# Attention, squared-ReLU layer and expert layer in one kernel: weight conversion from step 26, and some copies of transposed probabilities on VectorE

## The chip, the cores and the metric

The kernel runs on one core of one Trainium2 chip. The metric is the device time of one execution in microseconds, and the median over executions is what is compared. The engines are called as the profile calls them: PE is TensorE (PEld its weight loads), DVE is VectorE, ACT is ScalarE, POOL is GpSimd, and SP is SyncE, whose queue issues nearly all DMAs. Each of the engines works through its own instructions in the order in which they were written into its queue; a scheduler settles that order when the program is built.

## The reference

Three layers follow one another. The first is attention over 4 batches of 8 heads, 576 positions and 64 columns a head, where a block of 64 queries sees its own block of keys and the earlier ones. The second multiplies by `w_in`, squares the positive part and multiplies by `w_out`. The third sends each token to one of 8 experts.

```python
scores = scale * np.matmul(q, k.transpose(0, 1, 3, 2))
mask = block_i >= block_j                  # blocks of 64 positions
attn = np.exp(scores - max) / (sum + 1e-09)
x = np.matmul(attn, v)                     # (4, 8, 576, 64) -> 2304 tokens x 512
h = x @ w_in                               # 512 -> 2048
x = (s * np.maximum(h, 0) ** 2 + b) @ w_out
e = argmax(x @ w_gate + modality_bias[modality_id])   # 8 experts, 512 -> 1024 -> 512
out = gate * (np.maximum(x @ w1[e], 0) @ w2[e])
```

## The kernel before

**Attention.** A unit is a pair of heads of one batch: 16 units, each of 9 query blocks. `attention` is a generator that goes through 144 steps, one for each unit and block, and some steps more to drain. In a step it writes down the scores of one block (`scores`, lines 123 to 149: matmuls into a PSUM bank `sc`, the row maximum `nm` on DVE in line 142, the exponentials on ACT in line 147), the normalisation of the block before (`normalise`: the reciprocal `rc` on DVE, the product on POOL in line 160), and the transposition of the probabilities of a block five steps back (`p_transpose`: transposes on PE in line 179 into a bank `tp`, and a copy to the tile `pt` in line 185). `pv` multiplies `pt` by `v`, seven steps behind the scores; its results are copied on ACT (line 204) and stored to `xT_d` (line 207). At steps 4, 5 and 6 of a unit the next unit's q and k are transposed and split in a high and a low part.

**PSUM banks.** In the first 36 steps (units 0 to 3) attention has all eight banks: 4 for scores, 3 for transposes, 1 for `pv` (`BANKS_0`). From step 36 on it has 3, 2 and 1 (`BANKS_A`), and the second layer has the other two.

**Conversion of weights.** The weights come as 64-bit floats. The generator `convert` (line 352) brings the first half of `w_in` and `w_out` in, 16 chunks of 512 KB. Each time it is asked, it issues the load of one chunk (`load_f64`, line 320, on SP, two buffers `wr`), turns the chunk loaded before into 32-bit floats (`to_f32`: three DVE instructions on the tile `f`, lines 329 to 331), copies the chunk before that to its high part on ACT (line 364), and subtracts to get the low part of the one before that on POOL (line 335). It is asked 19 times in all, at the steps that the table `CONV` lists. Its instructions are held behind the step's last row maximum, exponential and product.

**Pieces of the second layer.** `_beside` gives out the work on the first six blocks of 256 tokens in 40 pieces: for each block one that loads the tokens, one for each `hidden` (24 matmuls of line 377, then relu, square and split) and two that project (line 392). A piece is written down when the step has reached `PIECE_0 + emitted * PIECE_D`, when enough chunks have been converted (11 for the first block, all 19 calls for the others) and when the block's tokens are finished.

```python
for _ in range(CONV.count(step)):
    ...
    converted += next(conv, 0)
while (emitted < len(plan) and step >= PIECE_0 + emitted * PIECE_D
       and converted >= 4 * NA[plan[emitted]] + 3 and done >= ...):
    next(pieces)
    emitted += 1
```

After attention the rest of the second layer (`after`) and the experts follow, with instructions that the change doesn't touch.

Of the kernel before, what the change touches and what calls it, by code (L numbers as in the profile page):

```python
# [20 lines left out]
def attention(nc, tc, ctx, ps, ident, q, k, v, xT_d):  # L21
# [140 lines left out]
    def p_transpose(u, blocks):  # L162
        i0 = blocks[0]
        grp = int(i0 >= 4)
        if i0 == 4 * grp:
            st[u]["pt", grp] = pt.tile(([P, 4, 2, P], [P, 5, 5, P])[grp], F32, name=f"pt{grp}", tag=f"pt{grp}")
        out = st[u]["pt", grp]
        nch = i0 // 2 + 1
        jobs = []
        if grp == 0:  # L170
            jobs.append(([(i, c) for i in blocks for c in range(nch)], out[:, i0:i0 + 2, 0:nch]))
        else:
            for c0, c1 in ((0, min(4, nch)), (4, nch)):
                if c1 > c0:
                    jobs.append(([(i0, c) for c in range(c0, c1)], out[:, i0 - 4, c0:c1]))
        for lst, o in jobs:
            t = ps.t.tile([P, 512], F32, name="tp", tag="t")
            for e, (i, c) in enumerate(lst):
                nc.tensor.transpose(t[:, e * P:(e + 1) * P], st[u][i][0][:, c * P:(c + 1) * P], ident)  # L179
            src = t[:, 0:len(lst) * P]  # L180
            if grp == 0:
                src = src.rearrange("p (i c n) -> p i c n", i=2, n=P)
            else:
                src = src.rearrange("p (c n) -> p c n", n=P)
            P_COPY(nc, i0)(o, src)  # L185
        for i in blocks:
            st[u].pop(i)

# [31 lines left out]
    def at(t):  # L220
        return seq[t] if 0 <= t < len(seq) else (None, None)

    done = 0
    for t in range(len(seq) + LP + 1):
        u, i = at(t - LT)
        if i in (1, 3):
            p_transpose(u, [i - 1, i])
        elif u is not None and i >= 4:
            p_transpose(u, [i])
        u, i = at(t)  # L230
# [15 lines left out]
        u, i = at(t - LN)  # L246
# [3 lines left out]
        u, i = at(t - LP)  # L250
# [22 lines left out]
NPBUF = 6  # L273
PTBUF = 1
BANKS_0 = (4, 3, 1)
P_COPY = lambda nc, i: nc.scalar.copy


class SquaredRelu:
# [211 lines left out]
NH_A = 1  # L491
BANKS_A = (3, 2, 1)
WB_ENG = lambda nc: nc.vector
CONV = [8 + 4 * n for n in range(19)]
PIECE_0 = 50
PIECE_D = 2.8
WA_ENG = lambda nc: nc.gpsimd
PASSES = ((0, 0), (0, 1), (1, 0))

# [653 lines left out]
def kernel(  # L1153
# [33 lines left out]
    with ExitStack() as c2, ExitStack() as early:  # L1187
# [6 lines left out]
        for step, done in enumerate(attention(nc, tc, c2, banks, ident, q, k, v, xT_d)):  # L1194
            if step == per:
                early.close()
                banks.open(c2, tc, 1, *BANKS_A)
                ffn.banks(c2, "a", NH_A)
            for _ in range(CONV.count(step)):
                with ExitStack() as behind:  # L1200
                    for i in banks.last.values():
                        behind.enter_context(tc.issue_after(i.ins))
                    converted += next(conv, 0)
            while (emitted < len(plan) and step >= PIECE_0 + emitted * PIECE_D
                   and converted >= 4 * NA[plan[emitted]] + 3 and done >= H // 2 * (1 + (plan[emitted] * TB + TB - 1) // S)):
# [58 lines left out]
```

## Time and profile before

| | us |
|---|---|
| median of 3 runs | 938.83 (936.92 to 939.79) |
| the profiled execution, its own time | 937.27 |
| its span in the profile | 935.6 |
| PE busy | 901.0 (96%) |
| DVE busy | 591.9 (63%) |
| ACT busy | 520.5 (56%) |
| POOL busy | 210.9 (23%) |

The busy times are of the whole span. Attention's units 0 to 8 take its first 150 us, the other units run beside the second layer up to 330 us, and from there on attention is over. A matmul counts as busy from its start to its modelled end, so that a PE that is busy is not a PE at its peak.

### The profile page before, as it was taken

The page shows a single profiled execution, that of the slowest core. Times are in us where ns is not written, and L with a number is a line of the kernel's source. Part 1 is how long each engine was busy: PE and PEld are TensorE (multiplying, and loading weights), DVE is VectorE, ACT ScalarE, POOL GpSimd, SP SyncE. Part 2 cuts the span into 40 slices and gives each one's busy share as a digit, 9 for nine tenths or more (in the row PEclk, how much of TensorE's full clock was granted, in tenths as well). Part 3 has the DMA queues.
Part 4 walks back from the last instruction along what each step waited for, and adds up shares of the span by engine and source line. Part 5 has one row for each costly group of instructions (what it writes and reads, how often), then busy time and mean ns, then how long its engine had stood idle before and what let it go on. Part 6 is the DMA issues. An engine that isn't in the chain of part 4 may idle for free. (4 is left out here: it accounts for less than half of the span.)

```text
span 935.6 us, 16290 instructions
## 1 busy us (share of the span) xinstructions
PE 901.0 (96%) x5529; PEld 722.5 (77%) x5529; DVE 591.9 (63%) x1368; ACT 520.5 (56%) x1105; POOL 210.9 (23%) x319
## 2 busy tenths in 40 slices
PE   7979999999999999999999999999989999999995
PEld 5766777788878788999998888888467776766774
DVE  5988976463645446777344444445768887686772
ACT  6878786575757543333223322222378786776763
POOL 4666665142333200000000000002121322121110
PEclk9999999999999999999999999999999999999998
DMA  6565553322320233445022222115263696537400
GB/s 146 153 161 135 162 157 76 90 59 66 79 74 27 71 102 102 136 143 195 23 68 68 69 68 68 46 46 200 71 228 116 234 384 231 207 123 273 158 25 25
DMA packets 109477, 113.79 MB, mean 122 GB/s; under 512 B 62679, under 2 KB 80617, under 8 KB 109387
## 3 DMA queue, kind: packets, MB, share of 16 engines
q1 hardware_dynamic: 105579, 100.74, 34.4%
q0 software_dynamic: 3808, 11.94, 3.6%
q8 instruction: 46, 0.75, 0.3%
q14 instruction: 44, 0.36, 0.1%
HBM read 143.58 MB, written 19.80 MB: 175 GB/s over the span
## 5 line engine op out<-in xcount | busy, mean ns | idle before, releaser
L377 PE MATMUL ph<-xh,wih 128*128 128x256 f32 x576 | 163.0, 283 | 0.0
L377 PE MATMUL ph<-xh,wil 128*128 128x256 f32 x576 | 162.5, 282 | 0.0
L377 PE MATMUL ph<-xl,wih 128*128 128x256 f32 x576 | 162.3, 282 | 0.0
L160 POOL TENSOR_TENSOR p<-p,rc 128x64 f32<-128x64 f32 (+2 forms) x144 | 112.0, 785 | 136.0 <-DVE rc L159 69.8
L381 ACT ACTIVATE r<-ph 128x512 f32<-128x512 f32 x72 | 43.0, 597 | 163.2 <-PE ph L377 138.0
L382 DVE SCALAR_TENSOR_TENSOR r<-r,sc 128x512 f32<-128x512 f32 x72 | 55.8, 775 | 93.5 <-ACT r L381 92.8
L377 PEld LDWEIGHTS ph<-xh,wih 128*128 128x128 f32 x576 | 109.2, 190 | 3.6 <-ACT r L381 0.9
L377 PEld LDWEIGHTS ph<-xl,wih 128*128 128x128 f32 x576 | 109.2, 190 | 2.2
L377 PEld LDWEIGHTS ph<-xh,wil 128*128 128x128 f32 x576 | 109.3, 190 | 0.1
L142 DVE TENSOR_REDUCE nm<-sc 128x1 f32<-128x288 f32 (+8 forms) x160 | 70.8, 450 | 55.1 <-PE sc L140 44.8
L147 ACT ACTIVATE p<-sc,nm 128x288 f32<-128x288 f32 (+8 forms) x160 | 80.6, 507 | 22.3 <-DVE nm L142 8.9
L902 DVE TENSOR_TENSOR w1l<-raw,w1h 128x1024 fp32r<-128x1024 f32 x60 | 72.2, 1225 | 28.6 <-ACT w1h L901 28.1
L392 PE MATMUL px<-woh,gh 128*128 128x512 f32 x200 | 81.5, 407 | 0.0
L902 DVE TENSOR_TENSOR w2l<-raw,w2h 128x1024 fp32r<-128x1024 f32 x64 | 74.9, 1218 | 6.6 <-ACT w2h L901 6.3
L392 PE MATMUL px<-woh,gl 128*128 128x512 f32 x200 | 78.6, 394 | 0.0
L392 PE MATMUL px<-wol,gh 128*128 128x512 f32 x200 | 78.5, 392 | 0.0
L910 POOL DMA_INDIRECT xr<-x_d,gidx_e x2 | 2.3, 1130 | 317.4 <-DMA raw<-in_moe_w_dram 317.1
L901 ACT CAST w2h<-raw 128x1024 fp32r<-128x1024 f32 x64 | 66.3, 1053 | 11.9 <-PE py L993 11.1
L385 ACT ACTIVATE gh<-r,sc 128x512 fp32r<-128x512 f32 x72 | 52.2, 724 | 34.6 <-DVE r L382 34.6
L179 PE MATMUL tp<-ident,p 128*128 128x128 f32 x400 | 66.0, 280 | 5.3 <-POOL p L160 3.9
L901 ACT CAST w1h<-raw 128x1024 fp32r<-128x1024 f32 x60 | 61.9, 1051 | 13.9 <-PE ph L978 9.8
L185 ACT COPY pt<-tp 128x512 f32<-128x512 f32 (+3 forms) x128 | 61.8, 499 | 8.9 <-PE tp L179 8.3
(279 smaller groups left out, 1970.5 us busy)
## 6 DMA issues: line engine op xcount, KB each, us to landing
raw<-in_moe_w_dram SPq DMA_DIRECT2D x172, 512.0 KB
xr<-xT_d SPq DMA_DIRECT2D x19, 512.0 KB
wr<-in_moe_w_in_dram SPq DMA_DIRECT2D x16, 512.0 KB
wr<-in_moe_w_out_dram SPq DMA_DIRECT2D x16, 512.0 KB
row<-part_d SPq DMA_DIRECT2D x20, 256.0 KB
x_d<-row SPq DMA_DIRECT2D x18, 256.5 KB
xT_d<-x SPq DMA_DIRECT2D x16, 288.0 KB
raw_q<-in_q_dram SPq DMA_DIRECT2D x32, 128.0 KB
```

Of the source, the lines that this page charges most:

```text
L142: ps.last["max"] = nc.vector.tensor_reduce(nm[:, e:e + 1], sc[:, 0:w], AX.X, ALU.max, negate=True)
L147: ps.last["exp"] = nc.scalar.activation(pr[:, k0:k0 + w], scs[e][:, 0:w], AF.Exp, bias=nm[:, 0:1], accum_out=sm[:, e:e + 1])
L160: ps.last["scale"] = nc.gpsimd.tensor_mul(pr[:, 0:n], pr[:, 0:n], rc.to_broadcast([P, n]))
L179: nc.tensor.transpose(t[:, e * P:(e + 1) * P], st[u][i][0][:, c * P:(c + 1) * P], ident)
L185: P_COPY(nc, i0)(o, src)
L377: nc.tensor.matmul(ph[:, e], self.wi[p][w][:, c, e * P:(e + 1) * P], x[a][:, c], start=(n == 0), stop=(n == 3 * KC - 1))
L381: nc.scalar.activation(r, ph, AF.Relu)
L382: nc.vector.scalar_tensor_tensor(r, r, self.sc[:, 0:1], r, ALU.mult, ALU.mult)
L385: nc.scalar.activation(gh, r, AF.Identity, bias=self.sc[:, 1:2])
L392: self.nc.tensor.matmul(px, g[a][:, e, t * P:(t + 1) * P], self.wo[p][w][:, e], start=(first and e == 0 and n == 0), stop=(last and e == 1 ...
L901: self.nc.scalar.copy(ws[0][c], r)
L902: self.nc.vector.tensor_sub(ws[1][c], r, ws[0][c].bitcast(F32))
```

## The change

Three things change, all of them in the tables. `CONV` asks for chunks at steps 26, 29, 32, ... 80 where it was 8, 12, 16, ... 80. `PIECE_0` and `PIECE_D` start the pieces at step 59, one in 2.5 steps, where it was step 50 and one in 2.8. And `p_transpose` gives the copies of three kinds of block (the pair that begins at 2, the blocks 5 and 7) to DVE in units 0 to 3; the others stay on ACT.

```diff
-            P_COPY(nc, i0)(o, src)
+            P_COPY(nc, u, i0)(o, src)
...
-P_COPY = lambda nc, i: nc.scalar.copy
+P_COPY = lambda nc, u, i: nc.vector.tensor_copy if u < 4 and i in (2, 5, 7) else nc.scalar.copy
...
-CONV = [8 + 4 * n for n in range(19)]
-PIECE_0 = 50
-PIECE_D = 2.8
+CONV = [26 + 3 * n for n in range(19)]
+PIECE_0 = 59
+PIECE_D = 2.5
```

The order of instructions on DVE in unit 2, before (`nm` is the row maximum, `rc` the reciprocal, `f` a chunk in conversion, `wr` the chunk as loaded):

```order
L142 TENSOR_REDUCE nm<-sc 128x1
L158 TENSOR_SCALAR rc<-sm 128x1
L159 RECIPROCAL rc<-rc 128x1
L329 TENSOR_SCALAR f<-wr 128x512
L158 TENSOR_SCALAR rc<-sm 128x1
L330 SCALAR_TENSOR_TENSOR f<-wr,f 128x512
L159 RECIPROCAL rc<-rc 128x1
L142 TENSOR_REDUCE nm<-sc 128x1
L331 SCALAR_TENSOR_TENSOR f<-wr,f 128x512
```

The same place of the changed kernel:

```order
L142 TENSOR_REDUCE nm<-sc 128x1 x2
L156 TENSOR_SCALAR rc<-sm 128x1
L158 TENSOR_SCALAR rc<-sm 128x1
L185 COPY pt_605<-tp 128x512
L159 RECIPROCAL rc<-rc 128x1 x2
L158 TENSOR_SCALAR rc<-sm 128x1
L142 TENSOR_REDUCE nm<-sc 128x1
```

The conversion is gone from units 1 and 2, and a copy out of a `tp` bank stands between the maxima. Counted over DVE's whole order, units 1 to 8 held 1, 3, 2, 2, 2, 3, 2 and 1 chunks (by their last instruction) before, and hold 0, 0, 2, 3, 3, 3, 3 and 2 now; the copies number 1 in unit 0, 3 in each of units 1 to 3, and 2 in unit 4, which finishes unit 3's blocks.

DVE at the start of unit 6 in the changed kernel, where the chunks stand closest:

```order
L331 SCALAR_TENSOR_TENSOR f<-wr,f 128x512
L158 TENSOR_SCALAR rc<-sm 128x1
L142 TENSOR_REDUCE nm<-sc 128x1
L159 RECIPROCAL rc<-rc 128x1
L158 TENSOR_SCALAR rc<-sm 128x1
L329 TENSOR_SCALAR f<-wr 128x512
L159 RECIPROCAL rc<-rc 128x1
L142 TENSOR_REDUCE nm<-sc 128x1
L330 SCALAR_TENSOR_TENSOR f<-wr,f 128x512
L158 TENSOR_SCALAR rc<-sm 128x1
L142 TENSOR_REDUCE nm<-sc 128x1
L331 SCALAR_TENSOR_TENSOR f<-wr,f 128x512
```

Nearly every maximum there now stands behind one instruction of a chunk.

SP's queue at the end of a unit, before (V of a later unit, the store of `xT_d`, and the weights' loads):

```order
L67 DMA raw_v<-in_v_dram 128x4x64 x2
L68 DMA raw_v<-in_v_dram 64x2x64
L207 DMA xT_d<-x 128x576
L320 DMA wr<-in_moe_w_in_dram 128x4x256
L320 DMA wr<-in_moe_w_out_dram 128x1024
```

and in the changed kernel:

```order
L68 DMA raw_v<-in_v_dram 64x2x64
L320 DMA wr<-in_moe_w_in_dram 128x4x256
L207 DMA xT_d<-x 128x576
L320 DMA wr<-in_moe_w_in_dram 128x4x256
L67 DMA raw_q<-in_q_dram 128x4x64 x2
L320 DMA wr<-in_moe_w_out_dram 128x1024
L68 DMA raw_q<-in_q_dram 64x2x64
L67 DMA raw_k<-in_k_dram 128x4x64 x2
```

Three weight loads now stand between two V loads, and the third, which needs a free `wr` buffer, stands ahead of a part of q and of k.

On PE, the order of both kernels holds 72 matmuls of line 377 and 24 of line 392 ahead of unit 9. In unit 9 there were 103 and 48, and there are 72 and 48 now.

## Rows read from the trace of the kernel before

**Rows 1.** The page, share of the span by engine.

```profile
PE 901.0 (96%) x5529; PEld 722.5 (77%) x5529; DVE 591.9 (63%) x1368; ACT 520.5 (56%) x1105; POOL 210.9 (23%) x319
```

**Rows 2.** Busy time, from unit 9 on: stretch, its length, each engine, clock, DMA.

```profile
150.06:188.77 38.71, 37.69 (x246) 31.14 (x246) 18.94 (x54) 19.89 (x53) 9.87 (x25) 1.00 0.29 77
188.77:330.00 141.23, 141.01 (x973) 116.55 (x973) 71.75 (x230) 89.93 (x263) 46.08 (x85) 1.00 0.22 63
```

**Rows 3.** Busy time by unit, units 1 to 8, then units 3 to 8 together.

```profile
core 0: us, PE busy (x) PEld busy (x) DVE busy (x) ACT busy (x) POOL busy (x), PEclk, DMA share, GB/s
...
21.58:34.23 12.65, 12.10 (x92) 9.27 (x90) 10.61 (x39) 11.24 (x41) 7.07 (x15) 1.00 0.47 93
34.23:50.63 16.40, 13.32 (x95) 9.95 (x94) 15.68 (x46) 13.23 (x45) 10.89 (x17) 1.00 0.73 219
50.63:64.66 14.03, 12.88 (x85) 10.03 (x83) 11.38 (x39) 11.84 (x41) 10.05 (x17) 0.88 0.45 114
64.66:81.21 16.55, 14.84 (x99) 10.53 (x100) 13.15 (x43) 13.79 (x46) 11.10 (x18) 1.00 0.55 146
81.21:97.56 16.35, 14.95 (x107) 11.66 (x107) 14.77 (x43) 13.48 (x44) 10.88 (x17) 1.00 0.71 200
97.56:119.67 22.11, 20.08 (x137) 15.98 (x133) 19.67 (x50) 16.46 (x48) 12.78 (x18) 1.00 0.57 155
119.67:134.96 15.29, 14.88 (x104) 10.56 (x103) 12.79 (x39) 13.26 (x44) 9.50 (x16) 1.00 0.41 128
134.96:150.06 15.10, 14.71 (x110) 11.53 (x107) 11.35 (x39) 12.64 (x44) 11.28 (x18) 1.00 0.53 129
...
50.63:150.06 99.43, 92.34 (x633) 70.30 (x631) 83.11 (x251) 81.48 (x257) 65.59 (x99) 0.98 0.54 147
```

**Rows 4.** The conversion's own busy time (tile f): length, DVE, ACT, POOL.

```profile
21.58:34.23 12.65, 2.29 (x3) 0.62 (x1) 0.00 (x0) 1.00 0.47 93
34.23:50.63 16.40, 8.30 (x11) 1.25 (x2) 3.20 (x2) 1.00 0.73 219
81.21:97.56 16.35, 6.43 (x8) 1.36 (x3) 3.51 (x3) 1.00 0.71 200
...
134.96:150.06 15.10, 3.13 (x3) 1.23 (x2) 3.71 (x3) 1.00 0.53 129
21.58:50.63 29.05, 10.59 (x14) 1.87 (x3) 3.20 (x2) 1.00 0.62 164
50.63:150.06 99.43, 29.15 (x35) 8.13 (x13) 19.69 (x14) 0.98 0.54 147
```

**Rows 5.** Copies out of PSUM by shape, ACT's and DVE's, whole span.

```profile
L185 ACT COPY pt<-tp 128x512 f32<-128x512 f32 x64 | 37.4, 593 | 6.6 <-PE tp L179 6.2
L185 ACT COPY pt<-tp 128x384 f32<-128x384 f32 x32 | 15.0, 483 | 0.8 <-PE tp L179 0.6
...
L625 DVE COPY gx<-gt 128x512 f32<-128x512 f32 x9 | 6.2, 684 | 0.7 <-PE gt L623 0.7
...
L1028 DVE COPY sxT<-pts 128x256 f32<-128x256 f32 x4 | 1.7, 416 | 0.0
```

**Rows 6.** The conversion's instructions: duration in ns, least, median and most; waits.

```profile
L330 DVE SCALAR_TENSOR_TENSOR f<-wr,f x32: 666/693/1708, 24.6 to 437.7; 128x512 int32<-128x512 int32 x32
L331 DVE SCALAR_TENSOR_TENSOR f<-wr,f x32: 674/692/1394, 26.0 to 438.4; 128x512 int32<-128x512 int32 x32
...
  DMA wr<-in_moe_w_out_dram: 1.6, 2
```

**Rows 7.** Timeline of a stretch in unit 4: start, length, engine, instruction, wait.

```profile
66.46 1.49 POOL L335 TENSOR_TENSOR wil<-f,wih 128x512 fp32r<-128x512 f32 x1
...
66.91 1.59 DVE L330 SCALAR_TENSOR_TENSOR f<-wr,f 128x512 int32<-128x512 int32 x1
...
68.42 0.34 DVE L142 TENSOR_REDUCE nm<-sc 128x1 f32<-128x192 f32 x1
...
69.42 0.45 PE L140 MATMUL sc<-kh,qh 128*128 128x384 f32 x1 [1.11 <-ACT p L147]
```

## The prediction

> **What bounds the kernel now.** I read the page's first part, then busy time by stretch, then the conversion's own share of each stretch, then single instructions. PE is busy for 96% of the span [rows 1], but that mean covers two regimes. From 188.77 us to the end of attention at 330 it is busy for 141.01 of 141.23 us, and from 150.06 to 188.77 for 37.69 of 38.71 [rows 2]. There PE has a backlog, and the second layer's matmuls fill every gap of attention. Whatever makes units 0 to 8 shorter by an amount brings the whole backlog forward by that amount, if the same matmuls are done by then; the order shows that they are (72 of line 377 and 24 of line 392 ahead of unit 9 in both). So the question is how long units 1 to 8 take, and the edit touches exactly these.
>
> Their lengths differ much [rows 3]: unit 1 takes 12.65 us, unit 2 16.40, although both do the same attention and neither holds a piece. What differs is the conversion: DVE spends 2.29 us on it in unit 1 and 8.30 in unit 2 [rows 4]. In unit 2 DVE is busy for 15.68 of 16.40 us, 95.6%, more than any other engine in any of these units. That is a unit bound by DVE. In unit 1 ACT has 11.24 of 12.65 (89%), DVE 84%, and PE 12.10, its waits between matmuls partly hidden in that figure. In units 3 to 8 DVE has 83.11 of 99.43 us (84%), ACT 81.48, POOL 65.59: no engine is full, and chains through all of them set the pace.
>
> How a chunk costs time is seen in unit 4 [rows 7]. DVE's second instruction on a chunk takes 1.59 us, beside a POOL instruction of 1.49; the row maximum behind it starts only at 68.42; its exponential frees a score bank late, and PE's next scores show 1.11 us of idle time. The cost is the delay of a maximum, not DVE's time as such.
>
> **The price of conversion.** The slope between units 1 and 2 is (16.40 - 12.65) / (8.30 - 2.29) = 0.62 us of unit for each us of conversion on DVE [rows 3, 4]. With three and two banks the nearest pair is units 8 and 5, each with about 24 matmuls of line 377: (16.35 - 15.10) / (6.43 - 3.13) = 0.38. So late conversion seems cheaper than early conversion. The bounds of this price: 0 if it all fits in the 16.32 us that DVE idles in units 3 to 8, and 1 if DVE is full.
>
> **Step 1: units 1 and 2 lose their conversion.** They give up 10.59 us of DVE and 1.87 of ACT [rows 4]. At 0.62 that is 6.6 us. The floor is the other bound: if no unit gets below unit 1's 12.10 us of PE, the two come to 24.2 where they took 29.05, and the gain is 4.85. ACT's floor lies lower, at 11.24 - 0.62 = 10.6. I take -6.3, near the slope, because PE's figure contains waits for ACT that the copies below shorten.
>
> **Step 2: units 3 to 8 take it over.** All 16 chunks are still finished before unit 9, and cost DVE 10.59 + 29.15 = 39.74 us in all. Units 3 to 8 thus get 10.59 us more. At 0.38 that is +4.0. The order supports a low price in one way: in unit 6 one instruction of a chunk stands between any two maxima, where unit 2 had up to two. At a price of 1 it is +10.6.
>
> **Step 3: the copies.** A copy of 512 columns takes 593 ns on ACT, one of 384 takes 483; on DVE 512 columns out of PSUM take 684 and 256 take 416 [rows 5], so that 384 lie half way, at 0.55 (an estimate). Per unit ACT loses 2 x 0.593 + 0.483 = 1.67 us and DVE gains 2 x 0.684 + 0.55 = 1.92. In units 1 and 2 DVE is left with 8.32 and 7.38 us of other work [rows 3, 4], so 1.92 stays under 11 us and is covered by PE's and ACT's own work; without that cover it would be 3.8 us in the two. ACT at about 9 us is then no bound there. In unit 3 and the start of unit 4, five copies put 3.2 us on DVE and take 2.8 off ACT; with both engines at 81 to 84% these about cancel. I put the step at 0, between -1.7 (ACT's part at 0.62) and +3.2 (DVE's part at 1).
>
> The Trainium skill (VectorE: DVE Perf Modes, Specifications) says that ScalarE sits closer to PSUM and VectorE closer to SBUF, which speaks against this step; the rows agree in direction, 593 ns against 684. It would add 12 x 0.09 = 1.1 us of work, which the sum has in the two figures already.
>
> **Step 4: the clock.** In unit 3 the granted clock is 0.88 on average over 14.03 us [rows 3], that is (1 - 0.88) x 14.03 = 1.7 us lost if PE had been full, at 1.2 GHz instead of 2.4 for some 3.4 us. It follows the unit in which PE was idle longest, 3.1 of 16.40 us. With unit 2 shorter this idle time goes. PE is not full there, so I take -0.9, between 0 (it comes back in a later unit) and -1.7.
>
> **Step 5: the pieces.** The same 40 pieces come, with the first block's moved from unit 5 and 6 to 6 and 7. Between 150 and 188.77 us PE idles for 1.0 us [rows 2]; 31 fewer matmuls in one heap in unit 9 can win no more than that. I take 0.
>
> **Step 6: the queue.** Three weight loads now lie between two V loads on SP, and DVE waited for a load in 2 of 32 cases, 1.6 us [rows 6]. Behind a late load stand DVE's maxima, and behind those everything. The loads are asked for three steps ahead of their use now, four before, and the third of a unit waits for a `wr` buffer. A step is about 1.8 us (99.43 us for 54 steps [rows 3]), so a load has about 5.5 us instead of 7.4. I take 0, since the scheduler puts the conversion of each about as far behind the stores as it was; at the 0.8 us of one such wait in each of units 4 to 8 it would be +4.0.
>
> **The sum.** -6.3 + 4.0 + 0 - 0.9 = -3.2 us. The profiled execution took 937.27 us, 1.7 outside its span included, and would come to 934.1. The median of the runs shown is 938.83, 1.56 above it, which gives 935.6 for the median.
>
> **The rivals.** With p as the price per us of late conversion, the difference is -7.2 + 10.59 p. A measurement of this kernel can tell about 0.3%, 2.8 us, from no change. So p under 0.42 is faster, p over 0.94 slower, and all between is the same.
>
> *The gain is given back.* If the price in units 3 to 8 is the 0.62 of units 1 and 2, moving chunks is worth nothing: -6.3 + 6.6 - 0.9 = -0.6, or 938.2. For it: unit 4 took 16.55 us with two chunks and no piece, more than unit 5 with more conversion, so that the 0.38 rests on a scatter of 1.3 us [rows 3]; attention then has fewer banks to hide a late maximum. The floor of 12.10 in step 1 leads to the same place (-4.85 + 4.0 - 0.9 = -1.8, or 937.1). Against it: DVE's idle time there is 16.32 us.
>
> *DVE fills up behind POOL: slower.* In units 3 to 7 every unit with three chunks stands where unit 2 stood, plus copies or the second layer's work. DVE would have 83.11 + 10.59 + 3.2 = 96.9 us of work. At unit 2's share of 95.6% that takes 101.4 us, 2.0 more than now; at unit 6's share, 19.67 of 22.11 or 89.0%, it takes 108.9, 9.5 more, and the sum is -6.3 - 0.9 + 9.5 = +2.3. At a price of 1, the whole added conversion on the path, it is +3.4, or 942.2. It decides from a share under about 88.6%. For it: line 330's instruction takes 666 ns at best and 1708 at most, the long ones beside POOL [rows 6, 7], and POOL's low parts now lie in the same units. The Trainium skill (GPSIMD Engine Reference, 1. Specifications) says that GpSimd shares its SBUF interfaces with VectorE and contends with instructions that have two SBUF inputs; lines 330 and 331 are such, and unit 4 agrees. By that rule a denser conversion stretches its own instructions. Against it: units 3 to 8 hold 14 of the 16 low parts already [rows 4], so POOL's share hardly rises.
>
> *A late load* gives 935.6 + 4.0 = 939.6, and counts with the same.
>
> **Chances and range.** Faster as summed 0.45; given back, or a late load, 0.32; slower 0.23. The likeliest case is 935.6, with a range of its own of 931.5 to 936.0. The low end takes unit 2's share of DVE (+2.0), the slope whole (-6.6), the clock whole (-1.7) and PE's last microsecond (-1.0): 7.3 us less, 931.5. The high end of the slower case is 942.2. The range runs from 931.4 to 942.2.
>
> **What would show it.** In the profile of the changed kernel units 1 and 2 should take about 11.4 us each, or 12.1 at the floor. DVE should be busy for about 10 us in each, and for 95 to 97 in units 3 to 8, which should last 102 to 104 us, and its share should lie at 92 to 95%; a share under 89% means that the slower rival holds. The granted clock should be 1.00 in units 1 to 8. Unit 9 should begin about 3 us earlier, at 147, and everything behind it should be moved by the same. DVE's idle time for `wr` should stay under 2 us. The prediction is wrong if units 1 and 2 stay above 12.5 us, if PE's waits for exponentials grow in units 4 to 7 by more than 4 us in all, or if the backlog from unit 9 on no longer fills PE.

## The result, and the profile after

The changed kernel takes 945.01 us (median of 4 runs, 944.82 to 945.94) against 939.16 of the kernel before beside it (4 runs, 936.92 to 939.79): a ratio of 1.0068, interval 1.0053 to 1.0082, so 0.7% slower. In the five groups of experiments the kernel before ran 100 times more, with medians of 940.0 to 940.9; against these the loss is 4 to 5 us. Ratios are estimated over all runs and need not be the quotient of two medians. The changed kernel's profiled execution took 944.82 us with a span of 943.1. The span before was 935.6, in an execution of 937.27 us, some 3 us below the median of those 100 runs; so up to 3 us of what the two profiles differ by is scatter.

The page's shares of the whole span answer to [rows 1]:

```profile
PE 905.6 (96%) x5529; PEld 727.5 (77%) x5529; DVE 597.7 (63%) x1380; ACT 516.5 (55%) x1093; POOL 210.8 (22%) x319
```

The twelve copies are in DVE's count (1380, 1368 before) and gone from ACT's. Nothing else shows at this level. Busy time by unit of the changed kernel, units 1 to 8, then units 1 and 2 together, 3 to 8 together, and unit 9; columns as in [rows 3]:

```profile
22.82:35.36 12.54, 11.97 (x89) 8.99 (x88) 9.85 (x38) 9.83 (x37) 6.50 (x13) 1.00 0.26 69
35.36:48.46 13.10, 12.47 (x93) 9.58 (x92) 9.77 (x38) 10.39 (x38) 6.87 (x15) 1.00 0.62 169
48.46:63.63 15.17, 12.07 (x88) 8.73 (x86) 12.22 (x43) 11.45 (x40) 8.64 (x16) 1.00 0.44 114
63.63:83.54 19.91, 17.02 (x97) 12.76 (x97) 17.45 (x48) 13.78 (x43) 10.72 (x17) 0.83 0.52 147
83.54:100.72 17.18, 14.33 (x88) 10.67 (x88) 16.07 (x45) 13.80 (x44) 12.87 (x18) 0.90 0.65 176
100.72:120.42 19.70, 17.67 (x120) 14.42 (x119) 17.57 (x47) 14.41 (x46) 14.21 (x19) 0.91 0.68 185
120.42:142.50 22.08, 21.53 (x136) 16.32 (x135) 18.95 (x48) 16.22 (x49) 11.27 (x18) 1.00 0.51 139
142.50:158.48 15.98, 14.73 (x110) 12.19 (x111) 12.82 (x43) 12.94 (x44) 12.54 (x18) 1.00 0.48 123
22.82:48.46 25.64, 24.44 (x180) 18.58 (x179) 19.62 (x76) 20.22 (x73) 13.36 (x27) 1.00 0.44 120
48.46:158.48 110.02, 97.35 (x634) 75.09 (x633) 95.08 (x269) 82.60 (x257) 70.25 (x101) 0.94 0.55 149
158.48:192.12 33.64, 33.61 (x215) 27.33 (x214) 17.40 (x51) 18.41 (x52) 9.91 (x25) 1.00 0.33 89
```

A unit is counted from its first exponential. Units 1 and 2 take 25.64 us where they took 29.05 [rows 4]: 3.4 less. Units 3 to 8 take 110.02 where they took 99.43 [rows 3]: 10.6 more, with the same number of matmuls (634 and 633). Unit 9 begins at 158.48 instead of 150.06, and from there on PE is full or nearly so in both (in unit 9 for 33.61 of 33.64 us, and before for 37.69 of 38.71 [rows 2]). The rest of the program, from unit 9 on, takes 943.1 - 158.5 = 784.6 us, where it took 935.6 - 150.1 = 785.5. So the loss lies in units 3 to 8, but for 1.2 us ahead of unit 1, which begins at 22.82 instead of 21.58. The granted clock, 0.98 over these units before, is 0.94, and units 4, 5 and 6 show 0.83, 0.90 and 0.91.

DVE is busy for 95.08 us there, as forecast (95 to 97), but that is 86.4% of the stretch. It is not full. The start of unit 4 shows a part of what happens instead. The timeline of the changed kernel, some of its rows (start, length, engine, instruction, and in brackets the idle time before it and what ended it):

```profile
59.67 0.38 SPq L320 DMA_DIRECT2D wr<-in_moe_w_out_dram  x1
...
63.51 1.33 DVE L329 TENSOR_SCALAR f<-wr 128x512 int32<-128x512 int32 x1 [1.37 <-DMA wr<-in_moe_w_out_dram]
64.10 0.49 PE L137 MATMUL sc<-kf,qf 128*128 128x128 f32 x2 [1.80 <-ACT p L147]
64.87 0.69 DVE L330 SCALAR_TENSOR_TENSOR f<-wr,f 128x512 int32<-128x512 int32 x1
65.61 0.69 DVE L331 SCALAR_TENSOR_TENSOR f<-wr,f 128x512 int32<-128x512 int32 x1
66.53 0.54 DVE L185 COPY pt<-tp 128x384 f32<-128x384 f32 x1
66.98 0.55 DVE L142 TENSOR_REDUCE nm<-sc 128x1 f32<-128x128 f32 x2
67.21 1.09 PE L179 MATMUL tp<-ident,p 128*128 128x128 f32 x4 [1.45 <-DVE pt L185]
67.36 0.37 ACT L147 ACTIVATE p<-sc,nm 128x128 f32<-128x128 f32 x1 [1.62 <-DVE nm L142]
```

DVE stands idle for a chunk's load, works through the three instructions of that chunk, and only then comes to the copy of unit 3's probabilities and to the maximum. PE waits 1.45 us for the copy (its bank `tp` is one of two), ACT 1.62 us for the maximum. PE's wait of 1.80 us for an exponential is not the copies' doing: conversion alone, without copies, has it too, with 1.70 us (last section). And the clock falls just then. Busy time of the same kernel around that place and in the two later dips:

```profile
60.00:64.80 4.80, 2.24 (x20) 1.55 (x19) 3.43 (x11) 3.13 (x11) 3.50 (x6) 1.00 0.96 292
64.80:71.60 6.80, 5.35 (x25) 4.95 (x23) 6.40 (x17) 3.50 (x11) 3.71 (x6) 0.50 0.60 155
71.60:80.00 8.40, 7.78 (x51) 4.93 (x49) 7.46 (x22) 6.61 (x20) 4.12 (x6) 1.00 0.21 43
88.70:92.10 3.40, 3.40 (x15) 2.83 (x16) 3.40 (x10) 1.92 (x8) 2.98 (x4) 0.50 0.88 239
105.80:109.20 3.40, 3.40 (x15) 3.31 (x14) 3.21 (x10) 1.83 (x6) 2.65 (x5) 0.50 0.92 260
```

PE was busy for 2.24 of 4.80 us, and is then granted 1.2 GHz for 6.8 us. Units 4 to 6 hold 6.8 + 3.4 + 3.4 = 13.6 us at that level; before, one stretch of 3.4 us in unit 3 was all that units 1 to 8 held.

PE has two more waits of over 1.2 us in units 3 to 8, 1.91 and 2.03 us, both longer than the one for the copy, and by then the last copy on DVE is over (at 69.03 us). The one in unit 6 (timeline of the changed kernel, some of its rows):

```profile
101.21 1.48 POOL L335 TENSOR_TENSOR wol<-f,woh 128x512 fp32r<-128x512 f32 x1
...
101.57 1.66 DVE L330 SCALAR_TENSOR_TENSOR f<-wr,f 128x512 int32<-128x512 int32 x1
...
103.16 0.15 DVE L159 RECIPROCAL rc<-rc 128x1 f32<-128x1 f32 x1
...
103.45 1.65 POOL L160 TENSOR_TENSOR p<-p,rc 128x576 f32<-128x576 f32 x1 [0.76 <-DVE rc L159]
...
105.15 0.66 PE L179 MATMUL tp<-ident,p 128*128 128x128 f32 x4 [2.03 <-POOL p L160]
```

A chunk's instruction, 1.66 us long beside one of POOL, stands ahead of a reciprocal; POOL's product waits for the reciprocal, and PE's transposes wait 2.03 us for the product. PE's waits for exponentials and for products in units 4 to 7, of the kernel before and then of the changed one (us in total, times, longest):

```profile
PE sc L140 <- ACT p L147: 2.4, 3, 1.1
PE sc L137 <- ACT p L147: 0.7, 1, 0.7
...
PE tp L179 <- POOL p L160: 0.5, 1, 0.5
```

```profile
PE tp L179 <- POOL p L160: 4.8, 3, 2.0
PE sc L137 <- ACT p L147: 1.8, 1, 1.8
```

The waits for exponentials have become shorter, and those for products have grown by 4.3 us. Over units 3 to 8 the waits for products are 0.7 us in the kernel before and 5.8 in the changed one. In two runs of the next section they are 1.1 us (the pieces alone) and 6.1 (conversion alone): they come with the moved conversion, and not with the copies. Over units 0 to 8 the sums are 3.9 and 7.1 us, as the kernel before has one such wait of 1.86 us at the end of unit 2, the unit that held three chunks.

### The profile page after: what moved, and what is told of

Same layout as the page of the kernel before. It is cut to its first block, busy times and chain, and to the rows that moved or that the text cites. A ratio compares the mean times of both kernels' runs of the same rounds, so it can differ in the third digit from the quotient of the medians.

```text
span 943.1 us, 16293 instructions
## 1 busy us (share of the span) xinstructions
PE 905.6 (96%) x5529; PEld 727.5 (77%) x5529; DVE 597.7 (63%) x1380; ACT 516.5 (55%) x1093; POOL 210.8 (22%) x319
## 5 line engine op out<-in xcount | busy, mean ns | idle before, releaser
L386 DVE SCALAR_TENSOR_TENSOR gl<-r,sc,gh 128x512 fp32r<-128x512 f32 x72 | 53.9, 748 | 19.5 <-ACT gh L385 19.4
```

Source lines behind the costliest of these rows:

```text
L386: self.low_last = nc.vector.scalar_tensor_tensor(gl, r, self.sc[:, 1:2], gh.bitcast(F32), ALU.add, ALU.subtract)
```

## Experiments

The first theory was that the slower rival of the prediction is right: conversion moved late costs its whole time, and the copies nothing. Its rival was that the copies cost.

**The parts alone.** One kernel has the copies only, the other moved conversion and pieces only.

```diff
# copies alone: against the changed kernel
-CONV = [26 + 3 * n for n in range(19)]      # and PIECE_0, PIECE_D as before
+CONV = [8 + 4 * n for n in range(19)]
# conversion alone: against the changed kernel
-P_COPY = lambda nc, u, i: nc.vector.tensor_copy if u < 4 and i in (2, 5, 7) else nc.scalar.copy
+P_COPY = lambda nc, u, i: nc.scalar.copy
```

> The kernel before with the copies of the change alone (three kinds of block on VectorE in units 0 to 3). The first theory, that the conversion moved into units 3 to 8 costs the time, expects no change here, 938 to 940.5 us. The rival, that copies on VectorE hold up the row maxima behind them, expects most of the 6 us: 943 or more, with units 1 to 4 longer by 1 us each.

> The change without its copies: conversion from step 26, a chunk in three steps, and the pieces from step 59; all copies on ScalarE. The first theory expects 944 to 947 us, units 1 and 2 at about 13 us each and units 3 to 8 about 9 us longer than before. The rival of the copies expects at most 941.

Copies alone: 945.17 us against 940.03, ratio 1.0055 (1.0039 to 1.0071). Conversion alone: 942.28, 1.0019 (1.0006 to 1.0033). The first theory fell. The copies, put at 0, cost 5 us on the kernel before, and moved conversion with its pieces 2.

**No conversion on DVE.** In both kernels the three instructions of a chunk are left out, and the weights that it converts are zeros (`zero` is a tile that POOL fills once).

```diff
-            f32 = raw and (self.to_f32(raw[0], raw[1].shape[1]), *raw[1:])
+            f32 = raw and (zero.rearrange("p (c n) -> p c n", c=raw[1].shape[1]), *raw[1:])
```

> The kernel before, in which the three VectorE instructions on each chunk during attention are left out (the weights that are used are zeros; loads, ScalarE's and GpSimd's parts stay). If these instructions stand on the path at a price of 0.4 to 1 us for each of their 39.7 us, attention gets shorter until PE's own chain is the floor, about 12.5 us a unit and 14 us of the second layer: some 15 us less, about 924, and no dip of the clock in units 3 to 6. If they were covered, 936 or more.

> The changed kernel with the same three instructions left out. The first theory expects it within 2 us of the kernel before without them (about 922 to 926), since only the copies and the place of loads and pieces are then left between the two. The rival of the copies, and one that blames loads or pieces, expects it 4 us or more above.

Zero weights send the tokens to other experts, so that the totals (953.31 and 958.21) don't compare with the other kernels', only the stretch up to unit 9. It begins at 138.4 in the kernel before without conversion (150.1 with it) and at 144.9 in the changed one (158.5). DVE's work on conversion thus costs 11.7 us for 39.74 in the one, 13.6 for 42.21 in the other: 0.29 and 0.32 a microsecond, nearly the same in both kernels. Units 3 to 8 of the two runs, the kernel before and then the changed one:

```profile
48.07:138.41 90.34, 87.58 (x641) 68.97 (x640) 59.94 (x220) 81.38 (x258) 61.81 (x106) 1.00 0.65 172
49.15:144.89 95.74, 90.05 (x634) 69.65 (x633) 60.90 (x221) 81.33 (x256) 63.26 (x102) 1.00 0.65 173
```

Up to unit 9, 6.5 us stay between the two kernels with no conversion on DVE in either, 5.4 of them in units 3 to 8. The two totals, which have the same zero weights, differ by 4.9 us, as much as the whole change costs. The granted clock is 1.00 in both rows. So the change costs about its full price without a chunk in DVE's queue and without a dip of the clock. What is left between the two are the copies, the pieces, the loads, and conversion's part on ACT and POOL.

**Which copy, and whether it is DVE's time.** One kernel keeps all copies on ACT and gives DVE twelve row maxima of the same size on a fixed tile instead; the others move the copies of some kinds of block only.

```diff
# idle reductions: before, behind P_COPY
+            if u < 4 and i0 in (2, 5, 7):
+                nc.vector.tensor_reduce(dull, idle[:, 0:len(lst) * P + 64], AX.X, ALU.max)
# some kinds: before, with
+P_COPY = lambda nc, u, i: nc.vector.tensor_copy if u < 4 and i in (2, 5) else nc.scalar.copy   # or (7,)
```

> The kernel before with all copies on ScalarE, and 12 reductions of a constant tile added to VectorE's queue, nearly where the copies stood and about as long; nobody waits for their results. If the copies cost by filling VectorE's queue, this costs the 5 us that the copies cost (943 to 946). If they cost because the copy itself comes late and the transposed probabilities, the product with v and its result on ScalarE wait for it, this costs at most 2 us (938.5 to 942).

> The kernel before with the copies of pair 2 and block 5 on VectorE in units 0 to 3, whose copies came 1.6 us later than ScalarE's did with all three; block 7 stays on ScalarE. The theory of the late copy expects nearly the whole cost, 943 to 946 us. A cost that goes by the number of copies gives two thirds, 942.5 to 944.

> The kernel before with the copy of block 7 alone on VectorE in units 0 to 3, which came no later than ScalarE's. The theory of the late copy expects no cost, 938 to 941 us, or a gain. A cost by the number of copies gives a third, about 941.5 to 942.5.

Against 940.23: idle reductions 941.70 (1.0018, 1.0004 to 1.0033); pairs at 2 and blocks 5 941.01 (1.0013, 0.9999 to 1.0026); blocks 7 939.53 (1.0006, 0.9993 to 1.0020). DVE's time alone makes about a third of the 5 us (0.4 to 3.1 us by the interval). The kinds do not add up to it: 0.13% and 0.06% against 0.55%. So no kind of copy alone accounts for it.

**The clock, held up by more matmuls.** Two more score matmuls a block in units 3 to 8 of the changed kernel, into the bank that the real ones then overwrite.

```diff
+            for _ in range(2 if 3 <= u <= 8 and i >= 2 else 0):
+                nc.tensor.matmul(sc[:, 0:max(w, 256)], qh[...], kh[...], start=True, stop=True)
```

> The changed kernel with two more score matmuls ahead of each block's in units 3 to 8; the scores overwrite them, so results stay, and PE gets some 2.4 us more work a unit, 14 us in all. If the half clock of 13.7 us in units 4 to 6 is a cause of its own, worth up to 5 us more than before, the dips go and the time falls to 940 to 943 or stays, though work was added. If the clock only follows the waits and costs little, the time rises by 3 us or more, to 948 and up.

957.42 us (1.0193, 1.0167 to 1.0218). The dips of units 3 to 8 fell from 13.6 to 3.4 us, but the units grew from 110.0 to 121.9 us: matmuls ahead of the scores lie on the chain, although PE has idle time. The clock can be had so, but the matmuls cost more than it gives back.

**A late copy and `pv`.** With the copies and without, `pv` written down a step later.

```diff
-LAGS = (1, 5, 7)
+LAGS = (1, 5, 8)
```

> The twelve copies on VectorE as in the changed kernel, conversion and pieces as before, and the product with v (pv) written down one step later (8 steps behind the scores where it was 7), so that a late copy has a step more before pv, and behind pv ScalarE's copy of x, wait for it. If the copies cost because pv and the ScalarE copy wait for a late copy, the cost of the copies (5.2 us with pv at 7) should fall to 1 us or less against the next kernel, which has the same pv and all copies on ScalarE. If they cost because VectorE's maxima stand behind a copy, or by the clock, about 4 to 5 us should stay.

> The kernel before with pv written down 8 steps behind the scores, and nothing else: the control of the run with the copies. Neither theory has a price for it; an estimate is 940, within 2 us of before.

948.48 us with the copies (1.0078, 1.0061 to 1.0095), 942.75 without (1.0016, 1.0004 to 1.0027). The difference is still 5.7 us. That `pv` and the ACT copy behind it wait for the late copy is not the cause.

**A third load buffer; conversion earlier.**

```diff
# third buffer: after
-        bufs = dict(raw=2, cv=3, xr=1, x=nx, r=nr, g=ng)
+        bufs = dict(raw=3 if ph == "a" else 2, cv=3, xr=1, x=nx, r=nr, g=ng)
# earlier: before
-CONV = [8 + 4 * n for n in range(19)]
+CONV = [6 + 3 * n for n in range(19)]
```

> The changed kernel with three buffers for the weights as loaded (wr) beside attention, where it has two, so that the third load of a unit can be issued a chunk earlier. If late loads on SP's queue are a part of the loss, VectorE's idle time for wr (1.8 us in unit 3, 0.2 later) goes and unit 9 begins 2 us or more earlier than 158.5; the time is about 943. If the order on VectorE alone makes the loss, nothing changes: 944 to 946.

> The kernel before with conversion moved the other way: a chunk in three steps from step 6 to step 60, with copies and pieces as before. By the prices that the runs gave (0.34 us of time per us of conversion in units 1 and 2, 0.71 in units 3 to 8), moving the last three or four chunks, 7 to 10 us of VectorE, out of units 7 and 8 into the first units is worth 2.7 to 3.7 us: about 937 against 940. If the price does not depend on the unit, 939 to 941; by the price of the prediction (0.62 early, 0.38 late) it is 2 us slower, 942.

The third buffer: 945.22, as the changed kernel. Its load for the start of unit 4 is still issued only at 60.71 us, and DVE waits 1.92 us for it, so that late loads were not tested by it. Conversion earlier: 945.68 (1.0050, 1.0034 to 1.0067) where the measured prices gave 937. These prices (0.34 early, 0.71 late) had been read between the kernel before and conversion alone, which also moves the pieces; the run of the pieces alone, further down, shows that this misled.

**Where the copies lie, and the pieces alone.** The copies in units 0 to 2 of the changed kernel; in units 0 and 1, or 2 and 3, of the kernel before; and the third part of the change alone.

```diff
-P_COPY = lambda nc, u, i: nc.vector.tensor_copy if u < 4 and i in (2, 5, 7) else nc.scalar.copy
+P_COPY = lambda nc, u, i: nc.vector.tensor_copy if u < 3 and i in (2, 5, 7) else nc.scalar.copy   # or u < 2, u in (2, 3)
# pieces alone: before
-PIECE_0 = 50
-PIECE_D = 2.8
+PIECE_0 = 59
+PIECE_D = 2.5
```

> The changed kernel with the copies on VectorE in units 0 to 2 only, so that nearly none of them lies in a unit with conversion. If the copies cost where they share VectorE's queue with conversion, units 3 and 4 together, 35.1 us in the changed kernel and 31.6 with conversion moved and no copies, fall back to about 32, and the time to 942 to 943 (a cost of 0 to 1 over moved conversion alone). If the copies cost by themselves, three quarters of the 2.9 us stay: about 944.5.

> The kernel before with copies on VectorE in units 0 and 1, where VectorE has 0 and 1 chunks of conversion. If they cost beside conversion alone, 940 to 941 (0 to 1 us over before); if they cost by themselves, half of the 5.2 us of all four units: 943.

> The kernel before with copies on VectorE in units 2 and 3, where VectorE has 3 and 2 chunks of conversion. If they cost beside conversion alone, nearly all of the 5.2 us: 944 to 945; if they cost by themselves, half: 943. With a mean granted clock over the runs as in the kernel before (0.990) instead of that of all twelve copies (0.987), the order on VectorE is the cause and not the clock.

> The kernel before with the third part of the change alone: pieces from step 59, one in 2.5 steps. The prediction puts it at 0: 940 to 941. If the 24 matmuls that come later (in units 6 and 7 where they stood in 5 and 6) were cover that PE lacks in unit 5, it is slower by 1 to 2 us, with a dip of the granted clock more in units 4 to 6, and moved conversion by itself costs nothing.

Against 940.52: the changed kernel with copies in units 0 to 2 only, 942.16 (1.0021, 1.0009 to 1.0033), as conversion alone without any copy (942.28). So by the medians the three copies of unit 3's blocks cost 945.01 - 942.16 = 2.9 us (4.4 by the ratios 1.0068 and 1.0021), and the other nine nothing, to within some 2 us. On the kernel before, the copies of units 0 and 1 (one chunk there) cost 1.6 us (942.15, 1.0017), those of units 2 and 3 (five chunks) 3.3 (943.86, 1.0037); together they give the 5 of all. So a copy costs most in the units that hold chunks. That the chunks are the reason is not shown by this: two of unit 3's three copies, those of blocks 5 and 7, also come after step 36, when there are two `tp` banks and no longer three, and no run tells the one from the other. The mean granted clock of this last run is 0.9875, as with all twelve copies (0.9873), so that it does not part order from clock either. Pieces alone: 940.86 (1.0000, 0.9989 to 1.0012).

The traces agree with the medians only in part. Of pieces alone, of conversion alone (which has the same pieces), and of the changed kernel with copies in units 0 to 2, in this order, units 1 and 2 together and units 3 to 8 together:

```profile
21.56:50.81 29.25, 25.48 (x184) 19.21 (x183) 26.42 (x84) 24.46 (x84) 18.15 (x31) 1.00 0.65 166
50.81:153.97 103.16, 96.15 (x654) 73.49 (x652) 84.04 (x258) 82.18 (x256) 69.01 (x109) 0.98 0.56 147
```

```profile
21.04:46.47 25.43, 24.40 (x176) 18.47 (x175) 17.77 (x70) 22.74 (x79) 13.55 (x29) 1.00 0.42 114
46.47:153.49 107.02, 95.39 (x638) 72.83 (x637) 92.89 (x265) 83.62 (x261) 68.66 (x101) 0.97 0.56 154
```

```profile
23.21:48.80 25.59, 24.41 (x180) 18.55 (x179) 19.64 (x76) 20.18 (x73) 13.34 (x27) 1.00 0.42 112
48.80:156.46 107.66, 96.20 (x634) 73.73 (x633) 93.61 (x266) 83.11 (x259) 69.75 (x101) 0.95 0.57 154
```

The pieces alone make units 3 to 8 longer by 103.16 - 99.43 = 3.7 us, but with 654 matmuls done by unit 9 where there were 633, and from unit 9 on that kernel takes 783.1 us, not 785.5. Line 377's matmuls follow one another at 0.12 us in the timeline of the kernel before (94.41, 94.53, 94.64 us), so that 21 of them are worth 2.5, and 1.2 of the 3.7 is left. Against this control moved conversion takes 29.25 - 25.43 = 3.8 us from units 1 and 2. It adds 107.02 - 103.16 = 3.9 to units 3 to 8, with 16 matmuls fewer done; at equal matmuls that is 5.8, an estimate. The copies of units 0 to 2 add 0.6 there, those of unit 3 another 2.4. Ahead of unit 1 the copies of units 0 to 2 add 2.2 (23.21 against 21.04), which their median does not show; the profiled execution of that run, 945.02 us, was the slowest of its ten.

With the copies of unit 3 on ACT, the start of unit 4 reads thus (timeline of the changed kernel with copies in units 0 to 2):

```profile
64.54 0.43 DVE L329 TENSOR_SCALAR f<-wr 128x512 int32<-128x512 int32 x1 [2.28 <-DMA wr<-in_moe_w_out_dram]
...
65.58 0.48 ACT L185 COPY pt<-tp 128x384 f32<-128x384 f32 x1
...
66.22 1.09 PE L179 MATMUL tp<-ident,p 128*128 128x128 f32 x4 [0.72 <-ACT pt L185]
```

The chunk's load is late here too (2.28 us of idle time), but the copy doesn't stand behind it, and PE waits 0.72 us for it. With the copies in units 2 and 3 of the kernel before, the same place reads:

```profile
67.17 0.43 DVE L329 TENSOR_SCALAR f<-wr 128x512 int32<-128x512 int32 x1 [3.00 <-DMA wr<-in_moe_w_out_dram]
...
69.04 0.54 DVE L185 COPY pt<-tp 128x384 f32<-128x384 f32 x1
...
69.73 0.63 PE L179 MATMUL tp<-ident,p 128*128 128x128 f32 x4 [2.60 <-DVE pt L185]
```

So these rows, and those of the changed kernel further up, show one chain: load, chunk, copy, bank, transposes. On ACT the copy does not wait for the chunk. How much of the copies' price this chain makes, the rows do not say; the two runs without conversion on DVE, where it cannot occur, say that it is not all.

**The loads a call ahead.** Two loads run ahead of their conversion, in three buffers; conversion stays at its steps. It was put into the changed kernel and into the kernel before.

```diff
-        raw = f32 = high = None
-        for c in chain((c for p in pairs for c in self.chunks(pool, p)), (None, None, None)):
+        raw = f32 = high = soon = None
+        for c in chain((c for p in pairs for c in self.chunks(pool, p)), (None,) * 4):
...
-            raw = c and (self.load_f64(c[0]), *c[1:])
+            raw, soon = soon, c and (self.load_f64(c[0]), *c[1:])
...
-CONV = [26 + 3 * n for n in range(19)]       # before: [8 + 4 * n for n in range(19)]
+CONV = [23 + 3 * n for n in range(20)]       # before: [4 + 4 * n for n in range(20)]
...
-                   and converted >= 4 * NA[plan[emitted]] + 3 and done >= ...
+                   and converted >= 4 * NA[plan[emitted]] + 4 and done >= ...
```

> The changed kernel with each chunk loaded one call before (two loads ahead of their conversion, three buffers wr, one call more and the first at step 23), and conversion at the same steps. In the runs with copies in unit 3, VectorE stood idle 1.4 to 3.0 us for a load of w_out with a copy of unit 3 behind it in its queue, and TensorE's transposes waited 1.5 to 2.6 us for that copy. If this late load is what makes the copies of unit 3 cost 2.9 us, the idle time for wr and TensorE's wait behind it at the start of unit 4 go, unit 9 begins at about 155.5 instead of 158.5, and the time is 942 to 943. If the chunk's own work ahead of the copy is the cause, 944.5 to 945.5.

> The kernel before with the same loads a call ahead (first call at step 4, conversion at the same steps, copies on ScalarE). VectorE waits 1.6 us for wr there, in units 4 and 5: if these waits are on the path, 938.5 to 939.5 against 940.5, faster than both kernels; if they are covered, 940 to 941.

The changed kernel with it: 943.23 us (1.0040, 1.0027 to 1.0052, against 940.16), between the two expectations; the wait of 1.45 us for the copy is gone, PE's waits for products in units 3 to 8 have fallen from 5.8 to 1.4 us, the wait of 1.80 for the exponential has become 2.13, DVE still waits 1.7 us for one load, and unit 9 begins at 154.95. The kernel before with it: 933.54 us (0.9923, 0.9901 to 0.9946). That is faster than both kernels, 0.8% under the one and 1.2% under the other, and four times what its idle time for `wr`, 1.6 us, had promised. Its units 3 to 8:

```profile
50.54:146.24 95.70, 88.93 (x631) 69.65 (x630) 83.45 (x253) 81.22 (x258) 66.22 (x102) 0.98 0.57 151
```

They take 3.7 us less than in [rows 3], and DVE's list of waits there holds no `wr` any more; but in units 1 and 2 it has one of 1.5 us that was not there before. The idle time for `wr` is 1.5 us in all where it was 1.6, so that it doesn't explain the 6.6 us, and what does is not shown. Nor does the edit bring the two kernels together: with it in both, the change costs 943.23 - 933.54 = 9.7 us.

## Why the prediction was wrong

**The bound** was read rightly: from unit 9 on PE is full (33.61 of 33.64 us in unit 9), and the end follows the start of that unit.

**Where the sum failed.** It gave -3.2; by medians the change costs 945.01 - 940.52 = +4.5. Of these 7.7 us, steps 1, 2 and 4 together make 4.6 (conversion alone takes 942.28 - 940.86 = 1.4 us more than the pieces alone, where -3.2 was forecast), step 3 makes 2.7 and the pieces 0.3.

**Step 1** (-6.3) was mis-sized: -3.8 in the run of conversion alone, -3.4 in the changed kernel. The slope of 0.62 between two units did not hold. Units 1 and 2 stopped at 25.4 to 25.6 us with PE busy for 24.4, which is the step's own floor of 24.2 in PE's busy time and one microsecond of gaps. PE's figure was said to contain waits for ACT that the copies shorten; with them ACT's work fell from 22.74 to 20.22 us, and the two units took 25.64 instead of 25.43.

**Step 2** (+4.0) was right or somewhat low in size: +3.9 as the traces stand, 5.8 at equal matmuls, or 0.55 for each of the 10.59 us instead of 0.38. So late conversion is not cheaper than early, which is the rival in which the gain is given back. The wait behind it was another than the prediction named. It followed a chunk to a late maximum, a late exponential and PE's scores [rows 7]; in units 4 to 7 PE's waits for exponentials fell from 3.1 to 1.8 us. What grew are PE's waits for POOL's products, from 0.5 to 4.8 us, behind a reciprocal that stands behind a chunk.

**Step 3** (0, at most +3.2) is the step whose reasoning failed. The copies cost 945.01 - 942.28 = 2.7 us on top of moved conversion (4.6 by the ratios 1.0068 and 1.0019), and units 3 to 8 show 3.0. The copy's own time was right: 681 ns for 512 columns and 534 for 384, against 684 and 550. The argument was not. It weighed the copies as work only (3.2 on DVE, 2.8 off ACT, both at 81 to 84%), and work on DVE makes about a third of their price, as the twelve reductions show. The rows show one reason more. Behind a chunk whose load is late, a copy of half a microsecond holds a `tp` bank and a maximum, and PE and ACT wait 1.45 to 2.60 us. The prediction had asked of the chunks what stands behind them, but not of the copies what stands ahead of them. That this makes the whole price is not shown, and the runs without conversion on DVE speak against it. The step's own bound of +3.2 was in neither end of the range; with it the upper end of 942.2 would have been 945.4.

**Step 4** (-0.9) had the wrong sign. The dip of unit 3 went, as forecast, and 13.6 us of half clock came in units 4 to 6.

**Step 5** (0) holds for the time, 940.86 against 940.52; by the stretches it moves 3.7 us into units 3 to 8 and 2.4 of them back out.

**Step 6** (0): DVE waited 2.0 us in all for `wr`, about as before, and the sum of such waits did not tell what moving the loads is worth. It took 6.6 us off the kernel before, where these waits were 1.6, and 1.8 off the changed one.

**The rivals.** The slower one, that DVE fills up behind POOL, came nearest: share under 88.6% (86.4), DVE's work 95 to 97 us (95.08), units 3 to 8 near 108.9 (110.02). Half of its mechanism is in the rows: instructions of a chunk run long beside POOL's, and PE waits behind them. The other half is not, since DVE is not full, and that the figures came so near is in part luck. Of the 10.6 us more in units 3 to 8 the pieces make some 1.2 at equal matmuls, conversion 5.8 and the copies the rest, 3.6, by single profiles. Its end of 942.2 us was too low by 2.8, and 1.4 of that is the baseline: the three runs it started from had a median of 938.83, the later 100 about 940.2. Of the prediction's own signs of being wrong the first came, units 1 and 2 above 12.5 us (12.54 and 13.10), and the second did not, since the waits that grew were not those for exponentials.

**The clock's part.** The mean granted clock of the changed kernel's runs is 0.9872, or 2 x 0.0128 x 943.2 = 24.1 us at half clock; the runs of the kernel before have 0.9906, or 17.7; conversion alone 19.0, copies in units 0 to 2 19.4. Within a kernel, from run to run, a microsecond more at half clock goes with 0.24 us more time (233 runs of 18 kernels, the two with zero weights left out); a PE that is full would lose 0.5. So the 6.4 us more go with 1.5 to 3.2 us of the loss. But the two kernels without conversion on DVE have no dip in units 1 to 8, and differ by as much. So the dips are not needed for the loss; what they add to it where they come is an estimate.

**Open.** What makes the copies' price is not settled: the queue behind a chunk, the two banks, or the order elsewhere. Nor is it settled why the kinds alone cost so little, and why the loss stays whole without conversion on DVE. That twelve copies cost 5.1 us on the kernel before and 2.7 to 4.6 beside moved conversion may be noise. Each edit also reorders what the scheduler writes into five queues, and single profiles lie up to 3 us off their kernel's median. A call every three steps also meets the same blocks of each unit, in the changed kernel block 8 among them, whose scores take two banks; both kernels with such a spacing and no copies on DVE were slower (942.28 and 945.68), but no run tells the spacing from the density.

## What to carry to other kernels

Before you move an operation to an engine that has time, look at what stands ahead of it in that engine's queue, and at which buffer it keeps from whom while it waits; a share of busy time says nothing on that. Follow what stands behind a long instruction through every engine: here the short reciprocal behind a chunk kept POOL, and POOL kept PE, while the prediction watched the maxima. A slope between two stretches that differ in one load is no price beyond the next engine's floor, so check the sum against that floor and believe the floor. Put the bound of every step into the range. And a load issued a step earlier is worth a trial even where the idle time for it is small: here it took 0.8% off one order and 0.2% off the other, for reasons that are not known.

## What the runs showed of the hardware

Most dips of the granted clock in units 1 to 8 begin right behind a long wait of PE. In the run of conversion alone the two largest waits in units 3 to 8 are these:

```profile
62.18 0.51 PE L137 MATMUL sc<-kf,qf 128*128 128x128 f32 x2 [1.70 <-ACT p L147]
...
82.02 0.66 PE L179 MATMUL tp<-ident,p 128*128 128x128 f32 x4 [2.75 <-POOL p L160]
```

The clock falls to 1.2 GHz at 62.5 and at 83.0 us. Not every such wait brings a dip: one of 1.54 us that ends at 102.0 us in the same run does not. In the changed kernel waits of 1.80, 1.91 and 2.03 us end at 64.1, 87.8 and 105.2, and the clock falls at 64.8, 88.7 and 105.8. Four transposes then take 1.09 us; they took 0.63 at full clock in the timeline of the copies in units 2 and 3. The Trainium skill (TensorE: Matmul & The Clock Gate, What's actually happening) says that the clock follows how busy the array has been lately; these rows agree. So such a wait is paid twice, once as idle time and once in the matmuls behind it.

DVE's work on the chunks grew from 39.74 to 42.21 us:

```profile
48.46:158.48 110.02, 42.21 (x48) 10.00 (x16) 22.98 (x16) 0.94 0.55 149
```

It is the changed kernel's row for the tile `f`, read as [rows 4]. All 16 chunks lie in this stretch, and an instruction of line 331 there took 1.81 us beside one of POOL's line 335, where 0.69 is usual. The growth goes with a call every three steps, early or late: the work is 42.81 us in conversion alone and 42.41 in conversion earlier, and 39.23 with the pieces alone, where the calls stay four steps apart.
